# A fused attention and feed-forward kernel: the first tile's loads in another order, with the next batch's attention placed anew between its products

## The chip, the core and the metric

The kernel runs on one core of one Trainium2 chip. The metric is the device time of one execution in microseconds; lower is better. The core has TensorE (PE in the profile; PEld is its weight load), VectorE (DVE), ScalarE (ACT), GpSimd (POOL) and SyncE (SP), which here only issues transfers. Sixteen DMA engines move the data.

## The reference, cut to what matters

Attention with a window of 32 positions on either side, then a feed-forward layer with the tanh form of GELU:

```python
batch, n_heads, seq, head_dim = (8, 8, 576, 64)      # q, k, v in float32
n_tokens, d_model, d_ff = (4608, 512, 2048)          # 4608 = 8 * 576

scores = 1 / sqrt(64) * q @ k.T
scores = where(abs(i - j) <= 32, scores, -1e9)
attn = softmax(scores)
x = (attn @ v).transpose(0, 2, 1, 3).reshape(4608, 512)
out = gelu_tanh(x @ w_in) @ w_out
```

## The kernel before

**Tiles.** The 4608 tokens are worked in nine tiles of 512 (the loop over `t`, L811). Tile t needs attention of batch t and a little of batch t + 1 (576 tokens are one batch and 512 are one tile), so while tile t is in the second product, the kernel works the attention of batch `b = t + 1`. Everything is multiplied in float16: inputs come as float32 into staging tiles and are cast by DVE, POOL or ACT.

**A tile's two products.** `ffn_in` multiplies xT by `w_in` into PSUM (four contractions, `dc` 0 to 3, for each of 16 column blocks), and `gelu` writes gT. In tile 0 the second product is `ffn_out_0`, 64 matmuls of 512 columns at L611, in the order of the list `ORDER_0`: entries (t4, fc), where t4 is one of four token blocks and fc one of 16 row blocks of `w_out`. The later tiles use a seven-product scheme (L637), whose sums DVE makes at L582.

**Tile 0's weights.** `w_in` comes in four blocks of 1 MB (`wi[0]` to `wi[3]`, each in two loads of 512 KB), `w_out` in four more (`wo[0]` to `wo[3]`), all on SP's queue at L208 and L212, into a ring of five staging buffers. Row blocks fc 4 to 7 of `w_out` come from `wo[1]`, 8 to 11 from `wo[2]`, 12 to 15 from `wo[3]`; each row block is a slice that is cast by itself in `cast_w` (L217). Batch 1's queries and keys come by `qk(h0)`, two heads at a time (256 KB of q and 256 KB of k, for one pair of heads), its values by `vs`, in chunks of 128 positions, its last 64 positions by `tails`. SP issues in the order of the program.

**Attention of batch 1 in tile 0.** A plan written by hand, `PLAN_0`, says ahead of which of the 64 matmuls which step is issued. `r` g: eight transposes of pair g on PE (L324, L326) and two copies, QT on DVE (L331) and KT (L332). `s` g: scores of pair g (L434) and the exponential on ACT (L446); -1 is batch 0's last positions. `m` g: the mask on DVE (L452). `n` g: the row sums of two pairs (L457) with logarithm and exponential on ACT. `p` g: the products with V of two pairs (L467). `x` g: the scaled result into xT on DVE (L502). `t`: batch 0's last query positions turned (L313). `w` g and `u`: casts of `wo[g]`. `d` c: a chunk of values copied to the shifted layout (L197). `c`: a combination of weights for the later tiles. The suffix `@0` or `@1` names which of two pairs of PSUM banks, S0 or S1, a step uses; a step waits until the one before it on the same pair has been read.

**Zeros.** `spin(n)` (L249) multiplies a tile of zeros n times. It is called several times in the opening, the last time with n = 3 just ahead of the first product of `ffn_in`.

**Batch 2.** At matmul 55 of tile 0 SP gets `load_qk(2)` (L173 to L178). In tile 1, DVE casts them (L359, L382), SP turns them by DMA (L362, L384), and then loads batch 2's values (L390), which POOL casts (L303) and DVE copies to the shifted layout (L192, L193) before TensorE uses them at L467.

Of the kernel before, what the change touches and what calls it, by code (L numbers as in the profile page):

```python
# [36 lines left out]
def cut(b):  # L37
# [12 lines left out]

PLAN_0 = {4: "r1@1", 8: "r2@0", 10: "s0@1", 11: "w1", 14: "s1@0", 18: "t-1@1", 21: "r3@1", 22: "m0 s2@0", 25: "s3@1", 26: "m1",
          29: "s-1@0", 30: "w2", 31: "m2", 32: "m3", 33: "n0@1", 36: "m-1", 38: "n2@0", 42: "d0", 43: "d1", 44: "v-1@1",
          46: "w3", 48: "d2", 50: "d3", 52: "x-1", 54: "p0@0", 55: "u3 p2@1 x0 x1", 56: "x2 x3", 60: "c1"}
PLAN_1 = PLAN | {10: "s0@0", 12: "s1@1", 33: "s2@0", 40: "v0@1 v1", 50: "x0", 53: "x1", 57: "s-1@1", 62: "s3@0 v2",
                 63: "m-1", 66: "m3", 73: "v-1@1", 76: "x2", 80: "x-1", 86: "v3", 90: "s4@1", 98: "m4"}
PLAN_1[16] = "m0 m1"
for i in (4, 44, 84, 91):
    del PLAN_1[i]  # L60
PAIR_1 = {17: slice(0, 4), 40: slice(4, 8)}

ORDER_0 = [(t4, 4 * w + i) for w in range(3) for i in ((0, 1, 3, 2) if w else (0, 2, 3, 1)) for t4 in (0, 1, 3, 2)] + \
          [(t4, 12 + i + j) for i in (0, 2) for t4 in (0, 3, 1, 2) for j in range(2)]


# [5 lines left out]
def kernel(  # L72
# [9 lines left out]
    nc = tc.nc  # L82
# [124 lines left out]
    def load_w_in(i, w, c0=0, c1=4):  # L207
        nc.sync.dma_start(w[:, c0:c1, :], w_in_v[:, c0:c1, 512 * i:512 * i + 512])  # L208
        return w
# [10 lines left out]
    qk, tails_0, vs = load_early(0)  # L220
# [3 lines left out]
    qk(4)  # L224
    qk(6)
    load_table(exp_set)
    def v_of_pair(g):
        for h in (2 * g, 2 * g + 1):
            nc.sync.dma_start(raws[0][3][:, :, h, :], v[0, h, 0:512, :].rearrange("(c p) d -> p c d", p=128))  # L229

    vs(4)
# [1 line left out]
        v_of_pair(g)  # L233
    wi = [stage_w()]
    load_w_in(0, wi[0], 0, 2)
    v_of_pair(3)
    load_w_in(0, wi[0], 2, 4)
    for i in range(1, 4):
        wi.append(stage_w())
        for c0 in (0, 2):  # L240
# [5 lines left out]
    def spin(n, width=512, ps=None):  # L246
        ps = psO.tile([128, 512], FP32, name="spin", tag="O") if ps is None else ps
        for _ in range(n):
            nc.tensor.matmul(ps[:, 0:width], idle[:, 0:128], idle[:, 0:width], start=True, stop=True)  # L249
# [491 lines left out]
    qk(0)  # L741
    wo = [load_w_out(0, stage_w())]
    qk(2)
    qk(4)

    finish(0, bank(0))
    finish(1, bank(1))
# [3 lines left out]
    spin(2, 512, s0[:, 1, :])  # L751
    values(2, nc.gpsimd.tensor_copy)
    finish(2, s0[:, 0, :])
    spin(3, 512, s0[:, 1, :])
    nc.gpsimd.tensor_copy(w_in16[:, 0, 0:512], wi[0][:, 0, :])
    nc.scalar.copy(w_in16[:, 1, 0:512], wi[0][:, 1, :])
    values(3, nc.vector.tensor_copy)
# [9 lines left out]
            ffn_in(0, n, dc, dc + 1)  # L767
    cast_w(wi[1], w_in16[:, :, 512:1024], (0, 2))
    cast_w(wi[2], w_in16[:, :, 1024:1536], (0, 2))
    tails_0("q")  # L770
    wo.append(load_w_out(1, stage_w()))
    qk(6)
    wo.append(load_w_out(2, stage_w()))
    vs(0, 1)
    wo.append(load_w_out(3, stage_w(), 0, 2))
    vs(2, 3, 4)
    load_w_out(3, wo[3], 2, 4)
# [20 lines left out]
    quarter(3, 2, 3)  # L798
    load_table(exp_set)
    cast_w(wo[0], w_out16[:, 0:4, :], (0,), (0, 2, 3, 1))  # L800
    cast_early(1, 1, split)
    cast_early(1, 2, (nc.vector, nc.vector))
    cast_tails(0, nc.gpsimd, even)
    def spare(i):
        pt = psS.tile([128, 2, 8, 128], FP16, name="pt", tag=f"S{i}")
        return pt[:, 0], pt[:, 1]
# [4 lines left out]
    for t in range(NT):  # L811
# [34 lines left out]
        for i in range(113 if t else 65):  # L846
            if t and i == (4 if t > 1 else 46) and b + 1 < B:
                nc.gpsimd.tensor_copy(after, KLs[b % 2][:, 3, 0:1])
                load_v(b + 1)
            for act in plan.get(i, "").split():  # L850
                kind, at = act[0], int(act[act.index("@") + 1:]) if "@" in act else None
                g = int(act[1:].split("@")[0])
                if kind == "w":
                    if g == 3:
                        cast_w(wo[g], w_out16[:, 12:16, :], cs=(0, 1), on_dve=(0,))
                    else:
                        cast_w(wo[g], w_out16[:, 4 * g:4 * g + 4, :], on_act=(1, 3))
                    if g > 1:
                        cast_v(1, 2 * g - 4)
                        cast_v(1, 2 * g - 3)  # L860
                    if g == 3:
                        cast_vt(1)
                elif kind == "t":
                    trans_tails(0, spare(at)[0], even)
                elif kind == "r":
                    if g == 3:
                        cast_early(1, 3, (nc.vector, nc.vector))
                    trans_pair(1, g, *spare(at), copy=nc.scalar.copy)
                elif kind in "np":
                    pair = psS.tile([128, 2, 512], FP32, name="ps_od", tag=f"S{at}")  # L870
                    for x in range(2):
                        if kind == "n":
                            sum_up(1, g + x, pair[:, x, :], groups[(1, g + x)])
                        else:
                            ods[g + x] = (pair[:, x, :], lts[g + x])
                            times(1, g + x, pair[:, x, :], groups.pop((1, g + x)))
                    if kind == "n":
                        n = size(1, g)
                        lts[g], lts[g + 1] = lt4[:, g, :], lt4[:, g + 1, :]
                        for x in range(2):  # L880
                            nc.scalar.activation(lts[g + x][:, 0:n], pair[:, x, 0:n], AF.Ln)
                        for x in range(2):
                            nc.scalar.activation(lts[g + x][:, 0:n], lts[g + x][:, 0:n], AF.Exp, scale=-1.0)
                elif kind == "u":
                    cast_w(wo[g], w_out16[:, 12:16, :], on_dve=(3,), cs=(2, 3))
                    cast_tails(1, nc.gpsimd)
                    load_qk(2)
                elif kind == "c":
                    if g == 1:
                        B12 = combine_w()  # L890
                    combine(g, nc.vector)
                elif kind == "s":
                    score(*group(g), at)
                    if t == 1 and g == 4:
                        load_table(gelu_set)
                elif kind == "d":
                    pair_chunk(b, g, nc.vector.tensor_copy)
                elif kind == "m":
                    mask(*group(g))
                elif kind == "v":  # L900
                    bb, gg = group(g)
                    o, d = weigh(bb, gg, at)
                    ods[g] = (o, invert(bb, gg, d))
                    if t and g < 0 and b + 1 < B:
                        load_vt(b + 1)
                    if t > 1 and g == (3 if att else -1):
                        load_table(gelu_set)
                else:
                    spread(*group(g), *ods[g])
            if t == 1 and i == 30:  # L910
                cast_vt(2)
                store(0, *later[0])
                store(0, *later[2])
            if t == 1 and i in PAIR_1:
                pair_v(2, nc.vector.tensor_copy, PAIR_1[i])
            if t == 0 and i < 64:
                ffn_out_0(*ORDER_0[i])
            elif t and i < 112:
                ffn_out(t, i)
# [36 lines left out]
```

## Time and profile before

| what | value |
|---|---|
| median of 5 runs | 302.14 us (301.5 to 302.68) |
| the profiled execution, its whole time | 301.9 us |
| its span, first to last instruction | 300.2 us |
| mean granted TensorE clock | 0.996 |
| busy PE / DVE / ACT / POOL | 288.5 / 193.5 / 194.5 / 91.4 us |
| HBM read / written | 36.70 / 9.44 MB |
| first product of tile 0 (L539) | starts at 19.42 us |
| first matmul of L611 | starts at 35.05 us |
| first product of tile 1 | starts at 58.61 us |
| first product of tile 2 | near 90.5 us |

Times inside the profile are counted from the first instruction of the span. In the timeline a row is start, duration, engine, line, operation, output<-inputs, shape, number of instructions, and in brackets the idle time of the engine before it and who ended it. Matmuls are pipelined: a matmul of 512 columns is drawn 0.38 us long, but the next one starts 0.215 us after it. The rest of the numbers come from this one profiled execution, whose own time is 0.24 us below the median.

### The profile page before, as it was taken

Reading aid. Unit: us, or ns where it says so; the run is one execution under the profiler, and the core shown is the slowest. Engines: PE = TensorE matmul, PEld = TensorE weight load, DVE = VectorE, ACT = ScalarE, POOL = GpSimd, SP = SyncE. Lnnn points to the kernel's source line nnn. Section 1 sums busy time; section 2 is a strip of 40 time slices with the busy share of each in tenths; the row PEclk is TensorE's granted clock in tenths of the full one; section 3 lists DMA queues with packets and bytes.
Section 4 is the critical chain, followed back from the end, with each engine's and each line's share of the span. In section 5 each row is a group of like instructions: output and inputs, shape, how many; then the busy total and the mean of one; then the engine's idle time right before and its main releaser. Section 6 shows DMA issues by size and latency. Waiting matters only on the chain.

```text
span 300.2 us, 7129 instructions
## 1 busy us (share of the span) xinstructions
PE 288.5 (96%) x2896; PEld 179.3 (60%) x2896; DVE 193.5 (64%) x436; ACT 194.5 (65%) x308; POOL 91.4 (30%) x142
## 2 busy tenths in 40 slices
PE   6889799999999999999999999999999999999993
PEld 2534344445774488548854885478547854784583
DVE  4652548796968686967696669766876635442452
ACT  4865769479785795669567956695678666606600
POOL 3425516301637060606080506050700050015000
PEclk9999999999999999999999999999999999999998
DMA  7999999999799999798979996999592031004013
GB/s 210 264 290 384 309 333 213 277 183 210 208 212 201 238 216 175 146 160 215 172 166 149 229 165 138 159 210 180 103 178 37 3 103 40 2 9 131 2 38 102
DMA packets 116486, 50.73 MB, mean 169 GB/s; under 512 B 97975, under 2 KB 110007, under 8 KB 116454
## 3 DMA queue, kind: packets, MB, share of 16 engines
q1 hardware_dynamic: 87396, 37.88, 61.5%
q0 software_dynamic: 27936, 11.35, 25.7%
q10 hardware_dynamic: 1122, 1.06, 1.1%
q8 instruction: 22, 0.36, 0.6%
q14 instruction: 10, 0.08, 0.1%
HBM read 36.70 MB, written 9.44 MB: 154 GB/s over the span
## 4 chain that ended last, share of the span: by engine, by line
PE 83%; DMA 9%; SPq 4%; DVE 2%; issue 0%; POOL 0%; ACT 0%
PE mm L637 33%; PE mm L539 21%; PE ph L539 16%; DMA wst<-in_moe_w_in_dram 4%; DMA wst<-in_moe_w_out_dram 4%; PE ps_s L434 3%; SPq L229 2%; PE ps_d L457 2%; PE ps_o L467 2%; DMA tr<-in_k_dram 2%; PE mm L611 2%; SPq L208 2%; PE py L611 1%; PE ps_od L457 1%; PE ps_od L467 1%; DVE xT L502 1%
## 5 line engine op out<-in xcount | busy, mean ns | idle before, releaser
L539 PEld LDWEIGHTS <-w_in 128*128 128x128 f16 x576 | 56.2, 98 | 66.1 <-issue 0.5
L539 PE MATMUL mm<-xT,w_in 128*128 128x512 f16 x304 | 74.7, 379 | 0.1
L547 ACT ACTIVATE gT<-mm 128x512 f16<-128x512 f32 x76 | 45.1, 597 | 40.0 <-PE mm L539 39.3
L539 PE MATMUL ph<-xT,w_in 128*128 128x512 f16 x272 | 68.2, 379 | 0.0
L601 POOL DMA_DIRECT2D out_dram<-y x55 | 32.7, 604 | 88.4 <-DVE y L666 78.1
L637 PEld LDWEIGHTS <-s 128*128 128x128 f16 x512 | 49.5, 98 | 6.0
L582 DVE TENSOR_TENSOR s<-gT 128x512 f16<-128x512 f16 x64 | 27.1, 423 | 36.3 <-ACT gT L547 36.3
L547 ACT ACTIVATE gT<-ph 128x512 f16<-128x512 f32 x68 | 37.9, 599 | 13.2 <-PE ph L539 13.2
L637 PE MATMUL mm<-t,s 128*128 128x256 f16 x376 | 45.1, 273 | 0.0
L637 PEld LDWEIGHTS <-gT 128*128 128x128 f16 x384 | 35.7, 98 | 6.7
L446 ACT ACTIVATE pe<-ps_s 128x960 f16<-128x960 f32 (+1 forms) x32 | 30.4, 975 | 10.4 <-PE ps_s L434 10.3
L637 PE MATMUL mm<-w_out,gT 128*128 128x256 f16 x256 | 33.2, 273 | 0.0
L97 ACT ACT_TABLE_LOAD x18 | 23.1, 1283 | 2.2 <-issue 1.9
L493 ACT ACTIVATE lt<-lt 128x480 f32<-128x480 f32 (+3 forms) x36 | 21.1, 586 | 1.1
L492 ACT ACTIVATE lt<-ps_d 128x480 f32<-128x480 f32 (+2 forms) x28 | 15.6, 555 | 9.4 <-PE ps_d L457 5.6
L452 DVE TENSOR_TENSOR pe<-pe,band 128x960 f16<-128x960 f16 x28 | 18.9, 698 | 1.0 <-ACT pe L446 1.0
L183 POOL DMA_DIRECT2D V<-in_v_dram x20 | 17.9, 913 | 1.1 <-PE mm L637 0.4
L467 PEld LDWEIGHTS <-V 128*64 128x64 f16 x520 | 13.9, 111 | 6.1 <-DVE V L193 1.7
L637 PE MATMUL mm<-t,gT 128*128 128x256 f16 x128 | 16.5, 273 | 0.0
L502 DVE TENSOR_TENSOR xT<-ps_o,lt 128x480 f16<-128x480 f32 (+5 forms) x26 | 13.4, 536 | 2.8 <-PE ps_o L467 2.7
L637 PE MATMUL mm<-w_out,s 128*128 128x256 f16 x120 | 14.4, 273 | 0.0
L582 DVE TENSOR_TENSOR s<-s,gT 128x512 f16<-128x512 f16 x32 | 13.6, 425 | 1.1
(110 smaller groups left out, 318.8 us busy)
## 6 DMA issues: line engine op xcount, KB each, us to landing
kr<-in_k_dram SPq DMA_DIRECT2D x31, 256.0 KB, 11.0
qr<-in_q_dram SPq DMA_DIRECT2D x6, 1024.0 KB, 8.3
wst<-in_moe_w_in_dram SPq DMA_DIRECT2D x8, 512.0 KB, 8.4
wst<-in_moe_w_out_dram SPq DMA_DIRECT2D x3, 1024.0 KB
V<-in_v_dram POOLq DMA_DIRECT2D x20, 128.0 KB, 8.3
qr<-in_q_dram SPq DMA_DIRECT2D x7, 256.0 KB, 10.1
out_dram<-y POOLq DMA_DIRECT2D x6, 192.0 KB, 6.1
vr<-in_v_dram SPq DMA_DIRECT2D x8, 128.0 KB, 5.5
```

Of the source, the lines that this page charges most:

```text
L97: nc.scalar.add_instruction(mybir.InstLoadActFuncSet(name=nc.get_next_instruction_name(), act_func_set_id=which, ins=[], outs=[]))
L183: nc.gpsimd.dma_start(V[:, c, :, :], v[b, :, 128 * c:128 * c + 128, :].rearrange("h p d -> p h d"))
L446: nc.scalar.activation(pe, ps[:, :, 0:w], AF.Exp, scale=SCALE)
L452: nc.vector.tensor_tensor(pe, pe, m.rearrange("k (o j) p -> k o j p", o=1).broadcast_to(list(pe.shape)), op=ALU.mult)
L467: nc.tensor.matmul(o[64 * h:64 * h + 64, cols].rearrange("d (j p) -> d j p", j=4)[:, :, p0 - q0:p1 - q0], Vs[b % 2][:, slot, 2 * pr + h, : ...
L493: nc.scalar.activation(lt[:, 0:n], lt[:, 0:n], AF.Exp, scale=-1.0)
L502: nc.vector.tensor_tensor(xT[:, g, pos:pos + e], o[:, done:done + e], lt[:, done:done + e], op=ALU.mult)
L539: nc.tensor.matmul(ph, w_in16[:, dc, fc * 128:fc * 128 + 128], xT[:, dc, t * 512 % RING:t * 512 % RING + 512], start=(dc == 0), stop=(dc = ...
L547: nc.scalar.activation(gTs[t][:, fc, :], phs[fc], AF.Gelu_apprx_tanh)
L582: nc.vector.tensor_tensor(dst, x, y, op=op)
L601: eng.dma_start(out_v[b, j, q0 + p:q0 + p + e, cols], yo[m:m + e, cols])
L637: nc.tensor.matmul(pys["apart"][:, 0:256] if apart else py[:, blk, :], lhsT, wino[w][:, f, :], start=(new and i % (8 if one else 16) == 0) ...
```

## The change

Four things change, all of them in the first 58 us of the span.

- Loads of batch 0: the last two heads of values, which stood together between the two halves of `wi[0]`, are each followed by a quarter of `wi[0]`, so its second half becomes two loads of 256 KB.
- Loads of batch 1 and of `w_out`: `wo[1]` moves ahead of the third pair's queries and keys; `wo[2]` is split into two loads of 512 KB, with the fourth pair's queries and keys and a chunk of values between; the next chunk of values follows the second half.
- `PLAN_0` and `ORDER_0` are written anew; the casts of the third and fourth pairs (`k`), the casts of the values (`e`) and the second half of `wo[2]` (`w5`) become steps of their own. The cast of the second pair's queries moves from POOL to DVE; the KT copies of the second and fourth pairs move from ACT to DVE; one slice of `wo[3]` moves from DVE to ACT.
- The call `spin(3)` ahead of the first product goes.

```diff
-PLAN_0 = {4: "r1@1", 8: "r2@0", 10: "s0@1", 11: "w1", 14: "s1@0", 18: "t-1@1", 21: "r3@1", 22: "m0 s2@0", 25: "s3@1", 26: "m1",
-          29: "s-1@0", 30: "w2", 31: "m2", 32: "m3", 33: "n0@1", 36: "m-1", 38: "n2@0", 42: "d0", 43: "d1", 44: "v-1@1",
-          46: "w3", 48: "d2", 50: "d3", 52: "x-1", 54: "p0@0", 55: "u3 p2@1 x0 x1", 56: "x2 x3", 60: "c1"}
+PLAN_0 = {4: "s0@0", 9: "r1@1", 14: "s1@0", 15: "w1", 16: "m0", 19: "k2", 22: "r2@1", 23: "m1", 25: "s2@0", 27: "t-1@1",
+          29: "w2", 31: "s-1@1", 33: "n0@0", 35: "e0", 36: "m2", 37: "k3", 38: "w5", 39: "m-1", 40: "r3@1", 43: "e1",
+          45: "s3@0", 46: "v-1@1 d0", 47: "w3 e2", 48: "m3", 50: "d1", 51: "n2@0 x-1", 52: "e3 e4 d2", 54: "d3 p0@0",
+          55: "u3 p2@1 x0 x1", 56: "x2 x3", 60: "c1"}
...
-ORDER_0 = [(t4, 4 * w + i) for w in range(3) for i in ((0, 1, 3, 2) if w else (0, 2, 3, 1)) for t4 in (0, 1, 3, 2)] + \
+ORDER_0 = [(t4, 4 * w + i) for w in range(3) for i in ((0, 2, 3, 1), (0, 2, 1, 3), range(4))[w] for t4 in (0, 1, 3, 2)] + \
...
-    v_of_pair(3)
-    load_w_in(0, wi[0], 2, 4)
+    for x in range(2):
+        v_of_pair(3, (x,))
+        load_w_in(0, wi[0], 2 + x, 3 + x)
...
     qk(2)
-    qk(4)
...
     finish(2, s0[:, 0, :])
-    spin(3, 512, s0[:, 1, :])
...
+    wo.append(load_w_out(1, stage_w()))
+    qk(4)
     tails_0("q")
-    wo.append(load_w_out(1, stage_w()))
+    wo.append(load_w_out(2, stage_w(), 0, 2))
     qk(6)
-    wo.append(load_w_out(2, stage_w()))
-    vs(0, 1)
+    vs(0)
+    load_w_out(2, wo[2], 2, 4)
+    vs(1)
     wo.append(load_w_out(3, stage_w(), 0, 2))
     vs(2, 3, 4)
     load_w_out(3, wo[3], 2, 4)
...
-    cast_early(1, 1, split)
-    cast_early(1, 2, (nc.vector, nc.vector))
-    cast_tails(0, nc.gpsimd, even)
+    cast_early(1, 1, (nc.vector, nc.vector))
...
-                        cast_w(wo[g], w_out16[:, 4 * g:4 * g + 4, :], on_act=(1, 3))
-                    if g > 1:
-                        cast_v(1, 2 * g - 4)
-                        cast_v(1, 2 * g - 3)
-                    if g == 3:
-                        cast_vt(1)
+                        cast_w(wo[g % 3], w_out16[:, 4 * (g % 3):4 * (g % 3) + 4, :], on_act=(1, 3),
+                               cs={1: range(4), 2: (0, 1), 5: (2, 3)}[g])
+                elif kind == "e":
+                    cast_vt(1) if g == 4 else cast_v(1, g)
+                elif kind == "k":
+                    cast_early(1, g, (nc.vector, nc.vector))
+                    if g == 2:
+                        cast_tails(0, nc.gpsimd, even)
...
-                    if g == 3:
-                        cast_early(1, 3, (nc.vector, nc.vector))
-                    trans_pair(1, g, *spare(at), copy=nc.scalar.copy)
+                    trans_pair(1, g, *spare(at), copy=nc.scalar.copy if g == 2 else nc.vector.tensor_copy)
...
-                    cast_w(wo[g], w_out16[:, 12:16, :], on_dve=(3,), cs=(2, 3))
+                    cast_w(wo[g], w_out16[:, 12:16, :], on_act=(3,), cs=(2, 3))
```

## The prediction, made before the changed kernel was run

> **What bounds the kernel now.** I read the page first, then the chain of waits, then the timeline of each engine up to 60 us, then the table of stretches and the DMA landings.
>
> ```profile
> span 300.2 us, 7129 instructions
> ...
> PE 288.5 (96%) x2896; PEld 179.3 (60%) x2896; DVE 193.5 (64%) x436; ACT 194.5 (65%) x308; POOL 91.4 (30%) x142
> ...
> PEclk9999999999999999999999999999999999999998
> DMA  7999999999799999798979996999592031004013
> ...
> q8 instruction: 22, 0.36, 0.6%
> ```
>
> TensorE is busy 96% of the span, so a gain can only come from its idle time or from zeros. The fourth line says that the DMA engines are full in the first half. The stretches show where TensorE idles:
>
> ```profile
> 35.00:42.50 7.50, 5.90 (x65) 2.87 (x65) 2.56 (x6) 5.51 (x9) 3.19 (x6) 1.00 1.07 327
> 42.50:58.60 16.10, 15.92 (x182) 7.03 (x182) 12.22 (x26) 10.62 (x21) 7.51 (x10) 1.00 1.04 251
> 44.50:46.50 2.00, 2.00 (x43) 1.06 (x42) 1.56 (x4) 1.11 (x2) 0.05 (x1) 1.00 0.47 93
> ```
>
> (stretch, length, busy PE, PEld, DVE, ACT, POOL, clock, DMA share, GB/s.) From 35 to 42.5 us TensorE lacks 1.6 us; after 42.5 almost nothing until the end. So the change lives or dies in 7.5 us. TensorE's rows name the waits, POOL's explain the largest:
>
> ```profile
> 18.77 0.81 PE L249 MATMUL ps_o<-KT 128*128 128x512 f16 x3 [0.86 <-DVE xT L502]
> ...
> 32.90 0.40 PE L326 MATMUL pt<-idn,k 128*128 128x128 f16 x4 [0.49 <-DVE k L296]
> ...
> 37.20 0.40 PE L324 MATMUL pt<-idn,q 128*128 128x128 f16 x4 [1.10 <-POOL q L296]
> ...
> 42.50 0.59 PE L611 MATMUL mm<-w_out,gT 128*128 128x512 f16 x2 [0.27 <-DVE w_out L217]
> ```
>
> ```profile
> 34.60 1.99 POOL L217 CAST w_out<-wst 128x512 f16<-128x512 f32 x3 [2.72 <-DMA wst<-in_moe_w_out_dram]
> 36.51 0.63 POOL L296 CAST q<-qr 128x512 f16<-128x512 f32 x1
> ...
> 54.57 0.87 POOL L217 CAST w_out<-wst 128x512 f16<-128x512 f32 x1 [0.71 <-DMA wst<-in_moe_w_out_dram]
> ```
>
> At 37.20 the second pair's turn waits for a q cast that stood behind three weight casts; at 42.50 the matmuls wait for wo[1], landed at 42.00. The last row is the final slice of w_out: it lands at 54.5, so L611's last eight matmuls cannot start before about 55.2, however early TensorE is. They now start at 56.63.
>
> **Opening, and the zeros: costed at 0.** Without the three zero products TensorE is free at 17.9 and the first w_in casts end at 18.17, so the first product moves from 19.42 to about 18.2. None of it survives. The first block's third quarter lands near 19.2 (between the landings before, 17.84 and 20.75), the last value head near 19.5; its DVE cast and copies (0.42, 0.29, 0.28) end at 20.5, batch 0's last products at 20.9, xT 0.7 later, against 22.48 now. The next quarter then meets wi[1], cast at 22.60 to 23.03 (it starts at 23.39 now): 0.35 us left. The turn at 32.90 eats that: its k cast (DVE, 32.41) follows the band copies (30.65 to 32.39), which follow a w_in cast at 30.30. And L611 starts with wo[0], landed at 34.55: at 35.05 before and after. This cover also works the other way: up to 0.5 us of delay in the opening stays hidden; beyond, it costs one for one. The two extra loads cost SP 0.5 to 0.9 us of issue (467 to 877 ns at L208), while SP waits for landings anyway.
>
> A rule that speaks against taking the zeros: by the Trainium skill, "TensorE: Matmul & The Clock Gate", Part 1, an idle window of about 3.4 us puts the clock at half until a like time of work has passed, an estimate of 1.7 us lost. In this trace the gaps of 0.86 and 1.10 us above stand in stretches of clock 1.00, and the hole left by the zeros is 17.9 to 18.2. I take 0; with the rule's loss the sum below would be +0.85 instead of -0.85.
>
> **The walk from 35.05 to the end of tile 0** (0.2155 us a matmul; a score step 0.34, a turn 0.51, from TensorE's rows). Matmuls 0 to 3, s0, 4 to 8: r1 at 37.33. Its q is cast by DVE at 35.64 (landing), its k at 36.90 to 37.33: the 1.10 us wait is gone. r1 ends at 37.85, its DVE copies (0.42, 0.68) near 38.95; matmuls 9 to 13 end there too, s1 follows at 39.0 (S0 is free when ACT, after its table load to 37.99, has done the 0.97 us exponential). Matmul 16 is reached at 39.8. wo[1] now follows pair 1's keys (36.87); 1 MB took 2.5 to 2.9 us (wo[1] 2.52, wo[0] 2.78), so it lands near 39.5 and DVE's cast ends near 39.9. Now that point is reached at 42.50 with one turn more behind it: 2.0 us gained. Third pair: keys land near 41.0 to 41.2, DVE casts them to 41.6, r2 near 41.4 to 41.95, QT on DVE, then KT on ACT to 43.05: s2 waits about 0.45. r3 at 48, s3 at 49.5, its exponential and mask to 51.5, n2 to 52.1, two logarithms (1.03 for the pair) to 53.15, which free S0 for p0; the last values (POOL at 52.15, DVE copy after) allow it at 53.35: p0 waits about 0.5 where it would not before. p2 ends at 54.9, matmul 55 at 55.1; the last slice of w_out is ready at 55.2 (POOL 0.62 to 0.87; ACT casts its neighbour). Eight matmuls: 57.0. DVE scales xT from 54.05 (2.35 for four), then frees the first bank (0.6): tile 1 starts near 57.1 instead of 58.61. **Gain 1.5 us**: 2.0, less 0.5 for new waits.
>
> Queues that steps are moved past. SP: the third pair's two loads go behind wo[1] and cost pair 3 about 2.5 us, which r2 at matmul 22 instead of 8 no longer needs earlier; wo[2]'s split adds one issue. POOL: the cast of batch 0's last queries leaves the place ahead of wo[1]'s slice and waits for its landing near 42.0, needed at matmul 27 (43.9); behind the casts of values, which wait for landings up to 53.18, stand only slices that land later still. DVE: behind the casts of pair 3, waiting to 41.2, stand r2's copy and a mask, neither needed before 41.9; behind d0 stands the first slice of wo[3], needed at matmul 48 (51.0). TensorE: behind s2 and p0, all that follows.
>
> Moved casts and copies, at 0 beyond what the walk counts: DVE is busy 2.56 of 7.50 and 12.22 of 16.10 us, so two KT copies of 0.68 and one 0.43 cast fit; ACT gives up two copies of 0.59 and takes 0.61. If that cover is gone, the price is 0.4 to 0.7 at s1 or s3.
>
> **What is late next.** Batch 2's transfers, behind the same bytes on the same full engines. Its keys land at 64.88 (trace), DVE casts them from 65.28 at a free moment; earlier is at most 0.4, and so it is for the transposes and values on SP behind them. Then:
>
> ```profile
> 76.71 0.75 POOL L303 CAST V<-qr 128x512 f16<-128x512 f32 x1 [0.24 <-DMA qr<-in_v_dram]
> ...
> 78.41 0.42 DVE L193 COPY V<-V 64x768 f16<-64x768 f16 x1
> ...
> 78.88 0.27 PEld L467 LDWEIGHTS <-V 128*64 128x64 f16 x12 [0.32 <-DVE V L193]
> ```
>
> The fourth chunk of V lands at 76.65. Moved by 0.4: POOL to 77.0, DVE's two copies (0.42 each) to 77.9, against 78.88: **1.0 of 1.5 survives**. In tile 2 the first key transposes of batch 3 land at 104.56 and are used at 104.86: 0.3 of room, plus what they move (0.4 with the loads, up to 1.0 with DVE's q casts and the stores): 0.7 to 1.0, **0.85** taken. Later tiles have over 1 us of room there (134.10 for 135.27; 163.98 for 165.69). Against the profiled execution (span 300.2, 1.7 around it, 301.9): 301.05. Its time is 0.24 below the median, so by the median 302.14 - 0.85 = 301.3.
>
> **A transfer cost that no row settles.** Loads of values have runs of 256 B. The stretch at 44.5 (share 0.47, 93 GB/s) is a hole with SP stuck on an issue (42.47 to 46.19) behind two chunks of values, while an instruction fetch is open: 22 such packets at 0.6% of 16 engines are 1.3 us each. By the Trainium skill, "Runtime: NRT & Kernel Launch", Instruction fetch mechanics, crossing a 16 KiB block is mostly hidden; here the hole is about 1.1 us of full transfer. By the rule, spreading the values changes nothing; by the row it could win up to 1.1. But mixing may cost: values with half of wi[0] took 2.9 us to 20.75 where 0.4 + 1.35 is the usual price (1.15 lost), and the last values with the last weights 3.8 to 54.5 where 2.75 is (1.05 lost). Bounds for all transfers: 1.1 earlier to 1.5 later. I take 0, since the bytes ahead of the last slice are the same.
>
> **The rivals.** (A) Likeliest, 0.35: as above, 301.3 (300.9 to 301.5). (B) The hole closes, 0.20: last weights and batch 2 land 1 us earlier, the walk gains up to 1.9 and keeps it: 300.3. For it: no two value chunks adjoin there. Against: a fetch still holds an engine. (C) The gain is handed back, 0.27: batch 3's transposes stay at 104.56, or the last slice lands 0.5 later: 0.3 gained, 301.8. For it: the full DMA line. (D) Slower, 0.18: mixing. The change puts values between weights in three more places; at 1.1 each and part hidden, transfers run 1.5 late, V's last chunk ends 1.1 later than now, TensorE resumes at 79.4 instead of 78.88, tile 2 adds some: 302.8. It decides from 1.0 us of lateness in batch 2's values.
>
> **How the numbers follow.** 0.2% (0.6 us) is about what a measurement of this kernel tells from no change. Faster is A and B, 0.55; same C, 0.27; slower D, 0.18. The range 300.2 to 302.8 leaves out the far halves of B's and D's spread, about 0.15.
>
> **What would show it.** Right: r1 near 37.3 with no wait for POOL, matmul 16 near 40, tile 1 from near 57.1, then new idle of 0.5 near 77.5 before V's products. Wrong: matmul 16 after 41; the last slice landing after 55.5 (D) or before 54 (B); tile 1's V with no wait (C and A too low); clock under 1.00 near 18 us; wi or wo[0] landing off by more than 0.5.

## The result, and the profile after

The changed kernel's median is 302.83 us in 43 executions, that of the kernel before, run beside it on the same chips, 302.49. The ratio is 1.0019, with a 95% interval of 1.0004 to 1.0033. (Some executions fall into a slower state of the device, and every ratio here is of the others. It is the record's own ratio, not the quotient of the two medians beside it, from which it differs by up to 0.2%.) Against 302.14 this is 302.7, where 301.3 was predicted: no gain. Nor is it shown to be a loss, since the unchanged kernel compared with itself gave 1.0019 (1.0001 to 1.0037) once and 0.9997 (0.9972 to 1.0021) another time. The reading is "no difference that this measurement can tell".

The page of the profiled execution after (302.69 us in all):

```profile
span 300.9 us, 7125 instructions
...
PE 289.0 (96%) x2893; PEld 179.7 (60%) x2893; DVE 196.0 (65%) x438; ACT 194.5 (65%) x307; POOL 90.3 (30%) x141
...
PE 70%; DMA 18%; DVE 5%; SPq 2%; ACT 2%; issue 1%; POOL 0%
```

TensorE is as busy as before. DVE is busy 2.5 us longer. In the chain that ended last, DMA's share is 18% instead of 9%, and DVE's 5% instead of 2%: it passes through more waits of TensorE for others. The table of stretches after (columns as before):

```profile
35.00:42.50 7.50, 6.84 (x84) 3.52 (x85) 4.72 (x9) 5.58 (x8) 2.45 (x4) 1.00 1.13 289
42.50:58.60 16.10, 14.97 (x178) 6.92 (x169) 12.39 (x24) 10.41 (x19) 5.77 (x9) 1.00 1.02 259
44.50:46.50 2.00, 2.00 (x26) 0.74 (x23) 1.75 (x4) 1.25 (x3) 0.80 (x1) 1.00 0.99 320
```

The first stretch has gained 0.94 us of TensorE work (5.90 to 6.84), and the second has lost 0.95 of it (15.92 to 14.97). The hole in the transfers at 44.5 to 46.5 is filled (share 0.99, was 0.47). TensorE's rows after show where the gain is made and where it goes:

```profile
36.45 0.39 PE L326 MATMUL pt<-idn,q 128*128 128x128 f16 x4
...
42.31 0.40 PE L436 MATMUL ps_s<-QT,KT 64*64 64x96 f16 x16 [0.48 <-DVE pe L454]
...
52.85 0.29 PE L469 MATMUL ps_od<-pe,V 128*64 128x96 f16 x6 [0.37 <-ACT lt L883]
53.48 0.25 PE L469 MATMUL ps_od<-pe,V 128*64 128x64 f16 x4 [0.34 <-DVE V L200]
54.10 0.48 PE L469 MATMUL ps_od<-pe,V 128*64 128x64 f16 x18 [0.37 <-DVE V L200]
...
55.73 0.59 PE L613 MATMUL mm<-w_out,gT 128*128 128x512 f16 x2
...
57.62 0.81 PE L541 MATMUL mm<-xT,w_in 128*128 128x512 f16 x3
```

The second pair's turn (36.45) has lost its wait for POOL's cast. But `p0` waits three times, at 52.85, 53.48 and 54.10, 1.08 us in sum. The first wait is for ACT's logarithms, the last two are for DVE's copies of values. The kernel before had no wait at `p0`:

```profile
54.91 0.65 PE L467 MATMUL ps_od<-pe,V 128*64 128x96 f16 x28
```

DVE's rows and POOL's just ahead of it, after the change, say why:

```profile
50.39 0.66 DVE L454 TENSOR_TENSOR pe<-pe,band 128x960 f16<-128x960 f16 x1 [0.32 <-ACT pe L448]
51.08 0.71 DVE L198 COPY V<-V 64x512 f16<-64x512 f16 x1
51.80 0.67 DVE L200 COPY V<-V 64x512 f16<-64x512 f16 x1
52.40 0.41 DVE L510 TENSOR_TENSOR xT<-ps_od,lt 128x256 f16<-128x256 f32 x1
52.83 0.29 DVE L198 COPY V<-V 64x512 f16<-64x512 f16 x1
53.14 0.28 DVE L200 COPY V<-V 64x512 f16<-64x512 f16 x1
53.45 0.29 DVE L198 COPY V<-V 64x512 f16<-64x512 f16 x1
53.76 0.28 DVE L200 COPY V<-V 64x512 f16<-64x512 f16 x1
```

```profile
47.67 0.61 POOL L305 CAST V<-vr 128x512 f16<-128x512 f32 x1 [0.50 <-DMA vr<-in_v_dram]
...
51.03 0.62 POOL L305 CAST V<-vr 128x512 f16<-128x512 f32 x1 [0.49 <-DMA vr<-in_v_dram]
51.72 0.60 POOL L302 CAST V<-vt 64x512 f16<-64x512 f32 x1
...
55.06 0.62 POOL L218 CAST w_out<-wst 128x512 f16<-128x512 f32 x1 [2.73 <-DMA wst<-in_moe_w_out_dram]
```

The data of the copies `d1` (51.08 and 51.80) was there from 48.3, when POOL had cast their chunk, but the plan issues them behind the mask `m3`, and the mask waits for ACT's exponential of the fourth pair until 50.39. The two copies then took 0.71 and 0.67 us instead of 0.28, beside POOL's casts, and everything that `p0` needs from DVE ended at 54.04.

The last of POOL's rows is a second thing that ends late in this execution. The last slice of `w_out` landed at 55.01 and was cast by 55.68, and the last eight matmuls, which need it, begin at 55.73. So here they could not have begun much earlier even with `p0` on time. This profile alone does not tell the two apart; the experiments do.

Not all of the first profile pair is an effect of the change. Tile 0's fill started at 34.06 in it (35.05 before), and in all fourteen profiles of this study the start lies anywhere from 33.66 to 36.09. So tile 0 is read below from its own first matmul of L613 (L611 before), called its first fill matmul: from there to the first product of tile 1 it took 23.56 us after, and 23.55 before. The 0.99 us by which tile 1 began earlier in this pair (57.62 for 58.61) came from the opening, and the rest of the kernel took it back: tile 2 began 0.43 earlier (90.09), tile 3 0.18 earlier (120.75), tile 4 0.83 later (152.18). TensorE's rows after at these points:

```profile
78.20 0.38 PE L469 MATMUL ps_od<-pe,V 128*64 128x64 f16 x12 [0.33 <-DVE V L194]
...
104.68 0.62 PE L436 MATMUL ps_s<-QT,KT 64*64 64x96 f16 x32 [0.17 <-DMA KT<-k]
...
136.11 0.62 PE L436 MATMUL ps_s<-QT,KT 64*64 64x96 f16 x32 [0.94 <-DMA KT<-k]
```

### The profile page after: what moved, and what is told of

Its sections match the earlier page's. It is cut to its first block, busy times and chain, and to the rows that moved or that the text cites. A ratio compares the mean times of both kernels' runs of the same rounds, so it can differ in the third digit from the quotient of the medians.

```text
span 300.9 us, 7125 instructions
## 1 busy us (share of the span) xinstructions
PE 289.0 (96%) x2893; PEld 179.7 (60%) x2893; DVE 196.0 (65%) x438; ACT 194.5 (65%) x307; POOL 90.3 (30%) x141
## 4 chain that ended last, share of the span: by engine, by line
PE 70%; DMA 18%; DVE 5%; SPq 2%; ACT 2%; issue 1%; POOL 0%
PE mm L639 30%; PE mm L541 15%; PE ph L541 13%; DMA KT<-k 6%; DMA wst<-in_moe_w_in_dram 5%; DMA kr<-in_k_dram 3%; PE ps_s L436 3%; PE ps_d L459 2%; PE ps_o L469 2%; DMA tr<-in_k_dram 2%; SPq L230 2%; DMA out_dram<-y 1%; PE py L613 1%; ACT gT L549 1%; PE mm L613 1%
## 5 line engine op out<-in xcount | busy, mean ns | idle before, releaser
L436 PE MATMUL ps_s<-QT,KT 64*64 64x128 f16 (+3 forms) x576 | 13.8, 216 | 1.9 <-DMA KT<-k 1.1
L436 PEld LDWEIGHTS <-KT 64*64 64x64 f16 x576 | 10.1, 106 | 8.5 <-issue 3.8
```

Of the source, the lines that this page charges most:

```text
L436: nc.tensor.matmul(ps[64 * half:64 * half + 64, h, 4 * n * r:4 * n * r + 4 * n].rearrange("k (j p) -> k j p", j=4)[:, :, p0 - q0:p1 - q0], ...
```

## The experiments

Q: DVE's queue ahead of `p0` sets the end of tile 0. W: the last slice of `w_out` sets it. S: two stores of tile 0's output delay batch 3's key transposes. H: a fixed cause hands the gain back in tile 3. J: the later transposes by DMA scatter from execution to execution. O: the opening or its zeros matter. D: mixed loads are slower. Each kernel was compared with the kernel before on the same chip. "Tile 0" is the time from its first fill matmul to the first product of tile 1, in one profile; "last slice" is when the last slice of `w_out` landed, counted from the same matmul (the end of its cast's wait for it). Both are in us.

| kernel | median, before beside it | ratio, 95% interval | tile 0 | last slice |
|---|---|---|---|---|
| before | 302.14 | | 23.55 | 19.47 |
| the change | 302.83, 302.49 | 1.0019 (1.0004 to 1.0033) | 23.56 | 20.95 |
| the change again | 302.70, 302.24 | 1.0016 (0.9991 to 1.0040) | 23.75 | 19.05 |
| before again | 302.33, 302.24 | 1.0019 (1.0001 to 1.0037) | 23.40 | 19.69 |
| before, third time | 302.14, 302.27 | 0.9997 (0.9972 to 1.0021) | 23.65 | 20.29 |
| plan alone | 302.64, 302.24 | 1.0019 (0.9996 to 1.0043) | 23.19 | 18.75 |
| opening alone | 302.42, 302.24 | 0.9996 (0.9973 to 1.0018) | 23.36 | 19.47 |
| before without zeros | 303.07, 302.27 | 1.0024 (0.9995 to 1.0054) | 23.69 | 20.33 |
| change, `d1` ahead | 301.58, 302.58 | 0.9964 (0.9938 to 0.9989) | 22.80 | 19.07 |
| change, stores later | 301.97, 302.58 | 0.9977 (0.9958 to 0.9997) | 23.57 | 20.30 |
| change, all three edits | 301.22, 302.58 | 0.9958 (0.9936 to 0.9980) | 23.13 | 19.67 |
| before, two edits | 301.66, 302.58 | 0.9959 (0.9936 to 0.9981) | 23.52 | 19.89 |
| all three, plan loosened | 300.98, 302.27 | 0.9977 (0.9946 to 1.0007) | 23.96 | 18.65 |
| all three, copies on ACT | 301.31, 302.04 | 0.9977 (0.9958 to 0.9997) | 22.54 | 19.08 |

**The changed kernel and the kernel before once more.** No edit.

> The changed kernel a second time, nothing edited. In its first profile tile 1 began 0.99 us earlier than in the kernel before, tile 2 0.43 earlier, tile 3 0.18 earlier and tile 4 0.83 us later, with a wait of 1.1 us for key transposes in tile 3. Theory H (handed back by a fixed cause): the early tile 0 shifts stores and transposes of batch 4 into each other each time, so the wait in tile 3 is again 0.8 to 1.4 us and the time is 0.1 to 0.4% above before. Theory J (scatter of the transposes' landings): tile 1 again begins near 57.6 and the wait for V in tile 1 is there again (0.4 to 0.6), but the waits for transposes move: another tile, or none; the time within 0.3% of before, of either sign.

> The kernel before a second time, nothing edited; its first profile has tiles 1, 2, 3, 4 beginning at 58.61, 90.52, 120.93, 151.35 and no wait for transposes. H: the same, no wait for key transposes over 0.2 us in tiles 2 to 7. J: tile 1 within 0.3 us of 58.6, but a wait of 0.5 us or more for key transposes in at least one of tiles 2 to 7, as room there was only 0.3 to 1.9 us. Its time against itself also shows how wide the interval of a null is.

> The kernel before itself, unchanged, as a second comparison of it with itself. If the first such comparison (1.0019, 1.0001 to 1.0037) was scatter: a ratio nearer to 1, within 0.2%. If comparing in this way carries an offset: again about 1.002, and every ratio here is to be read against that.

The changed kernel takes 23.75 for tile 0 again, and this time not because of the last slice, which lands 1.90 us earlier than in its first profile, well ahead of its use. DVE is late as before. TensorE's row at `p0` and POOL's cast of the last slice:

```profile
54.32 0.48 PE L469 MATMUL ps_od<-pe,V 128*64 128x64 f16 x18 [0.74 <-DVE V L200]
```

```profile
53.20 0.61 POOL L218 CAST w_out<-wst 128x512 f16<-128x512 f32 x1 [1.03 <-DMA wst<-in_moe_w_out_dram]
```

The unchanged kernel spans 0.9997 to 1.0019, and an interval (1.0001 to 1.0037) that leaves out 1 came from it too, so 0.2% is the floor of what can be told. It also shows the hand-back without any change: in its second profile the fill began at 33.66, 1.39 us earlier than in the first, and tile 2 began only 0.95 earlier (89.57). TensorE's rows of the kernel before, run again:

```profile
77.68 0.38 PE L467 MATMUL ps_od<-pe,V 128*64 128x64 f16 x12 [0.38 <-DVE V L193]
...
104.42 0.62 PE L434 MATMUL ps_s<-QT,KT 64*64 64x96 f16 x32 [0.44 <-DMA KT<-k]
```

At 104.42 it waits for the same key transposes as the changed kernel does, and in its third profile it waits 0.60 us for them. So the waits in tiles 1 and 2 are not peculiar to the change: for V the kernel before waited 0, 0.38 and 0.35 us in its three profiles and the changed kernel 0.33 and 0.28, for batch 3's keys 0, 0.44 and 0.60 against 0.17 and 0.50. That is scatter, as J has it. In tile 3 the changed kernel waited 0.94 us and then 0.12, where H forecast 0.8 to 1.4 again; the kernel before did not wait there.

One thing is not scatter alone. Batch 4's transpose of queries, behind which its keys land, took 10.2, 10.9 and 10.1 us from issue to landing in the three profiles of the kernel before, and 12.4 and 11.6 in the two of the change. Over all fourteen, the old plan has 10.1 to 10.9 in five profiles and 12.2 in the sixth (the one without zeros), the new plan 11.1 to 12.4 in all eight. SP and POOL issue the same transposes and stores in the same order there. What goes with the duration is where a packet of instruction fetch (16 KB, kind "instruction" among the DMA packets) falls. In the four profiles where it starts 2.4 to 3.1 us after the transpose is issued, the transpose takes 10.1 to 10.9 us. In the other ten it starts 8.1 to 9.7 us after the issue, the landing follows 2.4 to 2.7 us behind it each time, and the transpose takes 10.5 to 12.4 us, on the whole the longer the later the packet; the kernel without zeros is one of these. So the plan may matter here only by moving the place where the next block of the program is fetched. That the fetch causes the delay is not shown: both could follow from a third thing.

**The plan alone and the opening alone.**

```diff
 # plan alone = the changed kernel, with
-    for x in range(2):
-        v_of_pair(3, (x,))
-        load_w_in(0, wi[0], 2 + x, 3 + x)
+    v_of_pair(3)
+    load_w_in(0, wi[0], 2, 4)
...
+    spin(3, 512, s0[:, 1, :])
 # opening alone = the kernel before, with these lines the other way round
```

> The changed kernel with the opening of before: values and weights of batch 0 in the old order and the three zero products back; plan, order and later loads as changed. H and J: the opening is worth nothing or up to 0.9 us at L613's start (35.05 before, 34.06 after), so tile 1 begins between 57.6 and 58.1; if the opening's transfers made the 0.9 us, near 58.1. Theory O (the zeros were needed): this one is faster than the changed kernel by 0.2% or more.

> The kernel before with the new opening alone: values between halves of weights, no zero products; plan and later loads as before. If the opening moves the landings, L611 starts near 34.1 instead of 35.05 and the wait at the second pair's turn grows by as much, so that tile 1 begins at 58.2 to 58.6. H and J: the time within 0.2% of before. O: slower than before by 0.2% or more.

Neither differs from the kernel before by more than the floor. The plan alone gains its 2 us at matmul 16 (4.95 us after the first fill matmul, 7.45 before; one turn of 0.51 us moves behind that point) and ends tile 0 at 23.19, close to the old plan's 23.36 to 23.69. Its 23.19 flatters it: in this profile the fill began 2.34 us after `wo[0]` landed, where 0.50 to 0.55 is the rule in twelve of the fourteen, so that all later landings were early by comparison. The next experiment shows what held it up.

**Without the zeros.** The kernel before, with one line taken out.

```diff
-    spin(3, 512, s0[:, 1, :])
```

> The kernel before without its products of zeros ahead of the first product, nothing else changed. If the zeros are idle work in a stretch in which TensorE waits for the first landing anyway: first product at about 18.2 us, first fill matmul of tile 0 in the scatter of the kernels before (33.7 to 35.1), time within 0.2% of the kernel before. If the zeros hold the granted clock: executions with a window of half clock in the opening (3.4 us at 0.5, 1.0 to 1.1 us of time) come more often than in the kernel before (7 of 59 and 8 of 22 with zeros), and the time is 0.2% or more above it.

The interval leaves it open whether this is slower. Its profiled execution had its first product at 20.20, later than with the zeros (19.42), and the table of stretches shows a window of half clock there (columns as before, the clock third from the end):

```profile
14.00:18.28 4.28, 1.61 (x34) 0.93 (x34) 2.35 (x6) 2.00 (x3) 1.72 (x3) 1.00 1.01 260
18.28:21.69 3.41, 3.41 (x24) 1.24 (x23) 2.07 (x6) 2.87 (x4) 0.38 (x2) 0.50 0.90 263
```

But the plan alone, which keeps the zeros, had such a window from 16.23 to 19.64 in its profile. For the executions without a trace only the mean clock is on record. This profile has 0.993, the plan alone's 0.991, and all profiles without a window have 0.996 or more. Below 0.9955 lie 53 of 261 executions of kernels with the three zeros and 34 of 180 of kernels without. So the zeros do not prevent a loss of clock. Where in those executions it was lost is not known.

**The copy `d1` ahead of the mask.** The scaling `x-1` moves behind the copies as well.

```diff
-          45: "s3@0", 46: "v-1@1 d0", 47: "w3 e2", 48: "m3", 50: "d1", 51: "n2@0 x-1", 52: "e3 e4 d2", 54: "d3 p0@0",
+          45: "s3@0", 46: "v-1@1 d0", 47: "d1 w3 e2", 48: "m3", 51: "n2@0", 52: "e3 e4 d2", 54: "d3 x-1 p0@0",
```

> The changed kernel with the copy of the second value chunk put ahead of the last mask, and batch 0's last scaling behind the copies instead of among them. Theory Q (DVE's queue): in the changed kernel p0 waits 1.6 us because the mask of pair 3 (50.4) and, behind it, three value copies and one scaling run one after another on DVE to 54.0; so here p0 runs through by about 53.3, counted from L613's first matmul at 19.2 to 19.4 instead of 20.4 to 20.6 for matmul 54, and tile 1 begins 22.3 to 22.8 after that matmul instead of 23.6 to 23.7. Theory W (the last weights): the last slice of w_out lands too late anyway (55.0 in one profile, 53.2 in the other); tile 1 stays at 23.3 or more. In the total Q gives 0.1 to 0.9 us less than the changed kernel, because tile 1 and 2 hand part of it back.

DVE's last copy of values, then TensorE's `p0`:

```profile
53.39 0.28 DVE L200 COPY V<-V 64x512 f16<-64x512 f16 x1
```

```profile
53.77 0.65 PE L469 MATMUL ps_od<-pe,V 128*64 128x96 f16 x28 [0.37 <-ACT lt L883]
```

Tile 0 takes 22.80 us, 0.75 less than before, with the last slice landing at 19.07, as it did in the changed kernel's second profile, whose tile 0 took 23.75. (The profiled execution took 305.55 us, 4 us above this kernel's median, so only tile 0 is read from it.) The ratio moved further than this explains: from 1.0019 to 0.9964 is 1.7 us.

**The stores later.** Two of tile 0's stores (256 KB each), issued in tile 2 while SP issues batch 3's transposes, go to tile 7.

```diff
-                if t == 2 and fc in (8, 9):
+                if t == 7 and fc in (8, 9):
```

> The changed kernel with two stores of tile 0's output (256 KB each), which are issued in tile 2 among the key transposes of batch 3, moved to tile 7. Theory S (stores delay the transposes): batch 3's first key transpose lands 1 us or more ahead of its use instead of 0.04, and the wait of 0.2 to 0.5 in tile 2 is gone; the total 0.2 to 0.5 lower. Theory X (the transposes are slow by themselves): landing and wait in tile 2 as before the edit.

SP's row of the key transposes, from the timeline of the changed kernel:

```profile
97.17 5.09 SPq L386 DMA_TRANSPOSE KT<-k  x2
```

and of this one, with its scores after it:

```profile
97.09 3.20 SPq L386 DMA_TRANSPOSE KT<-k  x2
...
104.16 0.62 PE L436 MATMUL ps_s<-QT,KT 64*64 64x96 f16 x32
```

SP is through the two transposes 1.9 us sooner in this pair (over all profiles 2.6 to 4.0 us without the stores and 3.7 to 5.1 with them). The first of batch 3's keys land at 101.52, 2.64 us ahead of their use, where the kernels with the stores in tile 2 had 0.30 us at most or waited; the wait is gone. The landing is the clearer sign: counted from the first product of tile 2 it comes at 11.7 to 13.0 us in the five profiles without the stores, and at 14.0 to 15.0 in eight of the nine with them (16.6 in the execution of 305.55 us). S holds, and tile 0 is unchanged (23.57). Batch 4's keys are still waited for, 0.65 us.

**All three edits on the changed kernel, and two of them on the kernel before.** The two above, and batch 2's values loaded between its two key transposes instead of behind them:

```diff
-            if b == 2:
+                if b == 2 and pr == 1:
...
```

The loads of the values, below that line, move into the loop with it. The kernel with two edits has the stores and the values, but the old plan and opening.

> Both edits together, and batch 2's values issued between its two key transposes instead of behind both. If gains are handed back only at V in tile 1 (0.4 to 0.5) and at the transposes of batch 3, then neither wait is left, tile 2 begins 1.0 to 1.5 us earlier than in the changed kernel counted from L613's first matmul (54.7 to 55.0 instead of 56.0 to 56.2), and the total is 0.8 to 1.5 us below it, below the kernel before too. If a later wait takes it (batch 4 or 7's transposes), the total falls by less than 0.5.

> The kernel before with the two later edits alone (stores of tile 0 in tile 7, batch 2's values between the key transposes). Under the theory that the waits in tiles 1 and 2 only take what tile 0 gained, this gains little: 0 to 0.5 us below before, its tile 1 at 23.4 to 23.6 after L611's first matmul. It is the control for the edits together: their difference is what the new plan is worth once its p0 is free.

DVE's rows of the kernel with all three edits, then TensorE's:

```profile
51.21 0.64 DVE L454 TENSOR_TENSOR pe<-pe,band 128x960 f16<-128x960 f16 x1
...
53.42 0.28 DVE L200 COPY V<-V 64x512 f16<-64x512 f16 x1
```

```profile
51.34 0.59 PE L613 MATMUL mm<-w_out,gT 128*128 128x512 f16 x2 [0.33 <-DVE w_out L218]
...
53.80 0.65 PE L469 MATMUL ps_od<-pe,V 128*64 128x96 f16 x28 [0.37 <-ACT lt L883]
```

With `d1` ahead, DVE's copies end at 53.70, and `p0` runs in one piece, held by ACT's logarithms of `n2`, which end 0.04 us after DVE's copies. No wait of TensorE for V or for keys is left from tile 1 on, in this kernel or in the old plan with the two edits, and tile 2 begins 55.06 us after the first fill matmul (forecast 54.7 to 55.0). Its ratio is the lowest, 0.9958; but the old plan with the two edits has 0.9959, where 0 to 0.5 us of gain was expected of it and it gained about 0.9. That fits the waits of the kernel before in tiles 1 and 2, 0.82 and 0.95 us in its second and third profile, which these edits remove. So no profit of the new plan on top of them can be told.

The four ratios of 0.9958 to 0.9977 need care. They were measured on one chip, beside a kernel before that was slower (302.58) than on the other chips (302.04 to 302.27), and no unchanged kernel was compared with itself there. The copy `d1` and the stores both moved the ratio by more than their own waits amount to. A common offset of some 0.2% in these four is therefore not excluded, and their intervals overlap. That each of the four is faster than the kernel before is likely, but not shown.

**The plan loosened further.** The kernel with all three edits, with `p0` on the other banks, the cast of `w3` ahead of `d1`, and `x-1` back in its old place:

```diff
-          45: "s3@0", 46: "v-1@1 d0", 47: "d1 w3 e2", 48: "m3", 51: "n2@0", 52: "e3 e4 d2", 54: "d3 x-1 p0@0",
-          55: "u3 p2@1 x0 x1", 56: "x2 x3", 60: "c1"}
+          45: "s3@0", 46: "v-1@1 d0", 47: "w3 d1 e2", 48: "m3", 51: "n2@0 x-1", 52: "e3 e4 d2", 54: "d3 p0@1",
+          55: "u3 p2@0 x0 x1", 56: "x2 x3", 60: "c1"}
```

> The kernel with all three edits, and tile 0's plan of it loosened at two more points: p0 of batch 1 goes to the other pair of banks (at matmul 54, p2 and the two logarithms' products after it), so that it no longer waits for the two logarithms of n2 on ACT (0.53 us in the kernel with all three edits), and the cast of the last column of w_out's stage on VectorE stands ahead of the value copy e2 (0.49 us of wait at matmul 48). Theory Q (tile 0's end is set by what VectorE and ACT still owe at p0): no wait at p0, and tile 1 starts 22.3 to 22.7 us after the first fill matmul of tile 0 (23.13 with all three edits, 22.80 with d1 ahead alone, 23.56 in the changed kernel); time 0.2 to 0.8 us below the kernel with all three edits, so 300.4 to 301.0 beside a kernel before of about 302.4. Theory W (the last slice of w_out sets it, landing 19.5 to 21.4 after the first fill matmul): tile 1 stays at 22.8 or later and the matmuls before it wait for the DMA; time within 0.2 us of the kernel with all three edits.

My edit went wrong, and instructively. DVE's rows and TensorE's:

```profile
50.24 0.84 DVE L218 CAST w_out<-wst 128x512 f16<-128x512 f32 x1
51.11 0.75 DVE L198 COPY V<-V 64x512 f16<-64x512 f16 x1
51.88 0.60 DVE L200 COPY V<-V 64x512 f16<-64x512 f16 x1
52.40 0.64 DVE L454 TENSOR_TENSOR pe<-pe,band 128x960 f16<-128x960 f16 x1
```

```profile
53.09 0.39 PE L459 MATMUL ps_od<-pe,ones 128*64 128x480 f16 x2 [0.83 <-DVE pe L454]
...
55.05 0.48 PE L469 MATMUL ps_od<-pe,V 128*64 128x64 f16 x18 [0.37 <-DVE V L200]
```

The forecast of 22.3 to 22.7 missed. The wait at matmul 48 and the wait for ACT are gone, as meant, but cast and copies, slowed beside POOL, now stand ahead of the mask; it ends at 53.04, `n2` waits 0.83 for it, and tile 0 takes 23.96. What stands ahead of the mask delays `n2`, and what stands behind it delays `p0`.

**Work taken off DVE.** The kernel with all three edits, with the copies `d2` on ACT, in its gap ahead of the logarithms, `p0` on the other banks, and `x-1` ahead of the last copies:

```diff
-          45: "s3@0", 46: "v-1@1 d0", 47: "d1 w3 e2", 48: "m3", 51: "n2@0", 52: "e3 e4 d2", 54: "d3 x-1 p0@0",
-          55: "u3 p2@1 x0 x1", 56: "x2 x3", 60: "c1"}
+          45: "s3@0", 46: "v-1@1 d0", 47: "d1 w3 e2", 48: "m3", 49: "d2", 51: "n2@0 x-1", 52: "e3 e4", 54: "d3 p0@1",
+          55: "u3 p2@0 x0 x1", 56: "x2 x3", 60: "c1"}
...
-                    pair_chunk(b, g, nc.vector.tensor_copy)
+                    pair_chunk(b, g, nc.scalar.copy if t == 0 and g == 2 else nc.vector.tensor_copy)
```

> The kernel with all three edits, with work taken off VectorE ahead of p0 instead of reordered on it: the two shifted copies of the third chunk of values (d2, 0.6 us each there) go to ACT, which idles for 1.17 us ahead of the logarithms of n2; p0 of batch 1 goes to the other pair of banks, so that it does not wait for those logarithms (p2 follows on the first pair). Theory Q (VectorE's queue ahead of p0 sets tile 0's end): VectorE is done with the last copies near 53.2 instead of 53.70, p0 starts 0.4 to 0.6 earlier, tile 1 starts 22.4 to 22.8 after the first fill matmul (23.13 with all three edits, 23.96 with the plan loosened the wrong way), time 0.3 to 0.6 below the kernel with all three edits. Theory W (the last slice of w_out sets it): tile 1 at 23.0 or later, with the last eight matmuls waiting for a cast of w_out; time as with all three edits (ratio 0.996).

Its DVE rows, then TensorE's:

```profile
52.34 0.69 DVE L198 COPY V<-V 64x512 f16<-64x512 f16 x1 [0.18 <-POOL V L305]
53.05 0.28 DVE L200 COPY V<-V 64x512 f16<-64x512 f16 x1
```

```profile
53.34 0.65 PE L469 MATMUL ps_od<-pe,V 128*64 128x96 f16 x28
...
76.38 0.40 PE L436 MATMUL ps_s<-QT,KT 64*64 64x96 f16 x16 [0.66 <-DMA KT<-k]
```

`p0` starts at 53.34 without a wait, the moment DVE is done, and tile 0 takes 22.54, as Q said. W falls as the bound in this profile: nothing waits for the last slice. Two things were taken away at once here, DVE's copies and the wait for ACT's logarithms, so the gain of 0.59 us over all three edits (23.13) belongs to both. Yet the time did not follow, and the forecast of 0.3 to 0.6 us below the kernel with all three edits missed. Tile 1 begins at 57.03, 0.46 earlier than with all three edits, and tile 2 at 89.45 for 89.42: the wait at 76.38, for batch 2's second key transposes, which now stand behind the values, took it all.

## Why the prediction was wrong, point by point

**The walk of tile 0.** The first half was right, counted from the first fill matmul. `r1` waits for nothing (2.39 us after it, forecast 2.28), matmul 16 comes at 4.89 (forecast 4.75; 7.45 before), and `s2` waits 0.48 (forecast 0.45). The mask of the fourth pair ends at 16.99 (forecast 16.45), half a microsecond late. The step that failed comes next: "the last values (POOL at 52.15, DVE copy after) allow it at 53.35: p0 waits about 0.5 where it would not before". That is 18.30 after the first fill matmul. POOL was in time: its cast of the last chunk ended 17.59 after it (forecast 17.72). DVE's last copy ended at 54.04, which is 19.98 after it, 1.68 late. Of this the late mask explains 0.54, and the two copies of `d1` explain 0.81: they took 1.38 us beside POOL's casts, and 0.57 was the price taken. The remaining 0.33 is the queue itself: the term counted one DVE copy behind POOL, while three chunks of copies and the scaling `x-1` stood behind the mask, and the mask waits for ACT. The text put "Moved casts and copies, at 0 beyond what the walk counts", because DVE is busy 12.22 of 16.10 us. It is a queue with waits in it, so that share says nothing of the moment at which it is through. Matmul 55 came at 21.36 (forecast 19.85), so all 1.51 us are lost by then. Tile 0 was forecast at 22.05 and took 23.56: the whole gain of 1.5.

A second term was mis-sized in the profile shown: "the last slice of w_out is ready at 55.2", 20.15 after the first fill matmul. It was ready 21.62 after it, and would have taken nearly the whole gain by itself. But its landing varies, from 18.65 to 20.95 over the profiles of the new plan, and where it was early DVE was still the bound. At the same landing (19.05, 19.07 and 19.08) tile 0 takes 23.75 as changed, 22.80 with `d1` ahead, and 22.54 with `d2` on ACT and `p0` on the other banks; with more in front of the mask it takes 23.96, though the slice landed at 18.65. Two more profiles of the changed tile 0 give 23.56 and 23.57, so its scatter of 0.2 is small beside these steps. That DVE's queue ahead of `p0` cost tile 0 its gain is thus shown, each step by one profile.

**The opening, costed at 0.** Right, and for its reason: the first product came at 18.16 (forecast 18.2), the fill still began 0.5 us after `wo[0]` landed, and the opening alone gave 0.9996. Wrong in its firmness: "at 35.05 before and after" held neither for the kernel before, whose three profiles have 35.05, 33.66 and 34.42, nor for the change (34.06, 34.10).

**The clock.** The prediction weighed the rule of the Trainium skill ("TensorE: Matmul & The Clock Gate", Part 1) and took 0. As a difference between the two kernels this stands, 20% of executions with the zeros against 19% without. As a claim on the chip it was too sure: the window of half clock exists in both. In the two profiles that have it in the opening, the fill began 1.58 and 2.34 us after `wo[0]` landed, 1.1 and 1.8 later than elsewhere, against 1.7 by the estimate from the rule. Over the executions of the kernel before, the 177 with a mean clock over 0.9955 have a median of 302.12, the 17 from 0.990 to 0.9955, about one window's worth (half of 3.41 us is 0.6% of the span), 302.55, and the 25 lower still 303.70. So one window costs less in the median than the estimate, and most executions below 0.9955 lost more than one; no trace of such a one is kept. In the profile without zeros it follows a stretch in which TensorE mostly waits (busy 1.61 of 4.28 us in the rows above); in the plan alone TensorE was busy 2.98 of the 4.23 us ahead of it, as much as in the kernel before, which had no window (2.97 of 4.28 from 14.00). So the clock does not follow from these shares alone.

**What is late next.** The places were right, tile 1's V (0.33 us of wait) and batch 3's keys (0.17), but not the reason: the kernel before waits there too in two profiles of three, so they are not what an earlier tile 0 ran into. What made batch 3 late was its transposes running among stores, which the prediction had named as one of the things that could be moved, without a price of their own. "Later tiles have over 1 us of room" was wrong: it took one execution's landings as fixed. Batch 4's keys were waited for in both profiles of the changed kernel (0.94 and 0.12 us), and had 0.54 and 1.35 us of room in the kernel before run again.

**The rivals.** B: the hole at 44.5 to 46.5 did close (share 0.99), and yet the last slice landed no earlier: 55.01, where 54.5 was read before, or 20.95 for 19.47 from the first fill matmul. D: from the landing of `wo[0]` to that of the last slice, six profiles with the old order of loads took 19.97 to 21.91 us, mean 20.55, eight with the new one 19.16 to 21.46, mean 20.18. Mixing costs nothing that can be seen, and filling the hole won nothing that can be seen. C came true in its verdict, no difference that can be told, and the first profile shows both its signs: the first of batch 3's keys at 104.64, and the last slice 0.5 later. Its number (301.8, against 302.7) did not come true, and in the second profile, with the slice early, tile 0 was no faster; so what C names is not what held tile 0. D's number, 302.8, was met by luck: the lateness in batch 2's values from which it follows was not there (TensorE resumed at 78.20, not 79.4).

**Still open.** Whether the change is slower by a real 0.1 to 0.2%; whether the edits make the kernel faster by a real 0.2 to 0.4%; whether the place of the instruction fetch lengthens batch 4's transpose of queries; and what starts a window of half clock in a given execution. No run takes these apart.

## What to carry to other kernels

Where a plan moves work between engines, walk the receiving engine's queue in order, with what each instruction waits for, and price a copy beside its neighbour engines as the trace shows it there. A gain in one tile is only worth the room at the next landings, and that room must be taken from several executions. Here `d2` on ACT gained 0.46 us at tile 1 and lost it at the next key transposes, while two edits that only made room, with the old plan, came as far (0.9959) as the new plan with them (0.9958).

## What was not expected of the hardware

- A window of half clock of 3.41 us, seen in the opening in two of fourteen profiles, one with the three zeros and one without. About one execution in five (87 of 441) has a mean clock below 0.9955.
- DVE's copies of 64 x 512 took 0.28 to 0.29 us alone and 0.58 to 0.75 beside a cast on POOL, over the tile 0 of all fourteen profiles. The copy of the same shape on ACT took 0.62 us.
- With two stores of 256 KB among them, the first of two key transposes landed 14.0 to 15.0 us after the first product of its tile in eight profiles of nine, and without them 11.7 to 13.0 (101.52 instead of 104.64 in the pair shown).
- A DMA transpose of 10 to 12 us landed 2.4 to 2.7 us after a packet of instruction fetch had started, in each of the ten profiles in which that packet fell late.
